# First layers of a mixture of experts that end at 8-token steps inside unchanged tiles

## The chip, the core and the metric

The kernel is one program on one core of a Trainium2 chip. The metric is the device time of a launch in microseconds, the median of several runs. On a core, TensorE (PE in the profile, its weight loads PEld) multiplies matrices, VectorE (DVE), ScalarE (ACT) and GpSimd (POOL) do the rest, SyncE (SP) issues most transfers. Each engine works through its own queue in order.

## The reference

Attention over a window of 128 tokens and 4 sink tokens (4 batches, 8 heads, 768 tokens, head size 64) gives 3072 token rows of 512 numbers. Each row then goes to one of 16 experts, picked in two steps (a group of 4, then one of 4 in it), and comes out scaled by the product of two softmax weights:

```python
g_idx = np.argmax(x @ w_group, axis=1)
e_idx = np.argmax(xg @ w_expert[g], axis=1)
h = np.maximum(xg[mask_e] @ w1[g, e], 0.0)      # 512 -> 1024
ye = h @ w2[g, e]                                # 1024 -> 512
out[tok_idx] = combined[:, None] * ye
```

All of it is float32. On the inputs drawn, the experts get 382, 244, 475, 275, 270, 204, 188, 163, 157, 156, 150, 134, 108, 92, 54 and 20 tokens in the order of ranks that the kernel uses: rank 0 and rank 1 are picked early, from a part of the tokens; the others follow by falling count.

## The kernel before, in words

**Two phases.** Up to some 185 us the kernel computes attention and routing, and it begins the first expert. From there on it works through the experts, one group of `GROUPS` (L52) after another. This text is on the second phase.

**Capacities.** Rank r has room for `CAPT[r]` tokens (L47), multiples of 32. Its tokens are gathered by index from a table in memory (unused places point at row 0), turned by TensorE and kept as columns of the tile `xx`, a rounded part and a residual, T columns each, one behind the other. Stores are scattered by index; unused places have an index out of bounds and are not written. If an expert has more tokens than `capt`, the flag `nov` sends the excess to `overflow` (L1493), a loop behind the main work that reads whole weights again for each tile of up to 128 tokens.

**First layer (`layer1_wide`, L974).** For each of 8 slices f of the hidden units and 4 slices c of the input, the weights (`hi`, a rounded part, and `lo`, the residual; `whi` and `wlo` in the profile) are the stationary operand of 128 columns, and the tokens are the moving operand. So the tokens are what is streamed: T columns. Every matmul brings its own weight load. With T of 240 or more there are three matmuls for each f and c: hi with the rounded tokens, hi with the residual tokens, lo with the rounded tokens, 96 in all. With T below 240 (`comb`, L976) the first two are one matmul over 2T columns, for the two token parts lie side by side: 32 pairs of one matmul of 2T columns with `hi` and one of T with `lo`. ScalarE and VectorE then add the halves (`hc`), and split the result after the ReLU into two parts again (`split_h`, L955).

**Second layer (`layer2`, L1106).** Here the hidden values are the stationary operand (w columns, at most 128) and the weights are what is streamed: 512 columns, whatever w is. In the ranks of `FEW` (3, 4, 8, 9, 10, 11) the last 32 tokens go another way: `few_tokens` (L1089) multiplies them unsplit (`hq`), four stationary tiles of 32 columns side by side.

**What sets the order.** A planner that runs while the program is built (`spend`, `wjob`, `routing`) keeps a model clock and puts the conversions of weights (ScalarE makes `whi`, VectorE makes `wlo`, for each chunk of 512 KB) between the other work. `split_h` tells it how long VectorE takes, by the number of columns (`dve(0.1 + T / 960)`). The order is then fixed. Weights are fetched by SP into nine buffers, and SP waits for each to come free.

**Stages.** The first layers lie in the trace of before as follows, from the span's start in us: rank 1 at 193.06, rank 8 at 218.40, rank 2 in two parts (256 columns at 235.23, 224 at 258.53), rank 9 at 280.18, rank 3 at 297.26, rank 10 at 332.42, rank 4 at 350.15, rank 5 at 381.75, rank 11 at 404.31, rank 6 at 421.98, rank 7 at 454.29.

Of the kernel before, what the change touches and what calls it, by code (L numbers as in the profile page):

```python
# [9 lines left out]
F32 = mybir.dt.float32  # L10
# [4 lines left out]
AF = mybir.ActivationFunctionType  # L15
ALU = mybir.AluOpType
# [5 lines left out]
P = 128  # L22
# [4 lines left out]
DM = H * D  # L27
# [4 lines left out]
NFC = F // P  # L32
# [30 lines left out]
HC = 3  # L63
# [16 lines left out]
for _g in PARTS:  # L80
    _o = 0
    for _q in _g:
        _rem = _q["T"] % P
        _m = _q["T"] - _rem if _q["r"] in FEW else _q["T"]
        _q.update(o=_o, nt=(_q["T"] + P - 1) // P, s=_rem if _rem <= 64 and _m == _q["T"] else 0, plain=_q["T"] <= 64, m=_m)
# [59 lines left out]
def moe_attention(tc, kqT, vN, vS, nsw, wgx, w1, w2, out):  # L145
    nc = Pinned(tc)
    v = nc.vector
    with ExitStack() as top, ExitStack() as att:
# [167 lines left out]
        def late_consts():  # L316
            for t in sacc:
                nc.gpsimd.memset(t[:, :, :, 1], 1e-9)
            nc.gpsimd.memset(rdt, 1e-9)
            other_masks()  # L320
            nc.sync.dma_start(wsb, wgx.rearrange("(c p) n -> p c n", p=P))
            for j in range(2):
                nc.sync.dma_start(wsd[j * D:(j + 1) * D, :, j],
                                  wgx.rearrange("(c j p) n -> j p c n", j=2, p=D)[j])
            for r in range(NE):
                nc.gpsimd.memset(capt[:, r:r + 1], float(CAPT[r]))
                nc.gpsimd.memset(caps[:, r:r + 1], float(CAPT[r] // P))

        def tables():
            v.tensor_scalar(colm, col, -float(P), None, ALU.add)  # L330
# [622 lines left out]
                v.tensor_copy(gate[0:w], src[p:p + w, DM:DM + 1])  # L953

        def split_h(q, fs, src):  # L955
            T, o, s, m = q["T"], q["o"], q["s"], q["m"]
            hi = hx[:, fs, o:o + m]
            nc.scalar.activation(hi, src[..., 0:m], AF.Relu)
            dve(0.1 + T / 960)
            yield  # L960
            if m < T:
                v.tensor_scalar(q["hq"][:, fs], src[..., m:T], 0.0, None, ALU.max)
            for a, z, d in ((0, m - s, m + s), (m - s, m, s)):
# [8 lines left out]
            return wt[k]  # L972

        def layer1_wide(q):  # L974
            T, o, r = q["T"], q["o"], q["r"]
            comb = T < 240  # L976
            lag = []
            if q["m"] < T:
                q["hq"] = yp.tile([P, NFC, 32], F32, name="hq", bufs=2)
            for f in range(NFC):  # L980
                ph = ps_h.tile([P, 512], F32, name="ph")
                fs = slice(f * P, (f + 1) * P)
                for c in range(NDC):
                    hi, lo = weights(1, r, c)
                    st, sp = c == 0, c == NDC - 1
                    if comb:
                        if sp:
                            nc.tensor.matmul(ph[:, 0:T], lo[:, fs], xx[:, c, o:o + T], start=False, stop=False)
                        nc.tensor.matmul(ph[:, 0:2 * T], hi[:, fs], xx[:, c, o:o + 2 * T], start=st, stop=sp)
                        if not sp:  # L990
                            nc.tensor.matmul(ph[:, 0:T], lo[:, fs], xx[:, c, o:o + T], start=False, stop=False)
                    else:
                        nc.tensor.matmul(ph[:, 0:T], hi[:, fs], xx[:, c, o:o + T], start=st, stop=False)
                        nc.tensor.matmul(ph[:, 0:T], hi[:, fs], xx[:, c, o + T:o + 2 * T], start=False, stop=False)
                        nc.tensor.matmul(ph[:, 0:T], lo[:, fs], xx[:, c, o:o + T], start=False, stop=sp)
                src = ph[:, 0:T]
                if comb:
                    src = yp.tile([P, 224], F32, name="hc", bufs=HC)[:, 0:T]
                    nc.scalar.copy(src, ph[:, T:2 * T])
                    v.tensor_tensor(src, ph[:, 0:T], src, ALU.add)  # L1000
                lag.append(split_h(q, f, src))
                if len(lag) > 1:
                    drain(lag[0])
                    lag.pop(0)
                next(lag[-1]) if not comb else None
                us = T / 200 + (0.24 if comb else 0.18)
                pop_todo()
                state["freed"] += 4 if q["last"] and f == NFC - 1 else 0
                yield us
            drain(lag[0])  # L1010
# [5 lines left out]
                    raise RuntimeError("weights out of order")  # L1016
            return held[k][0]

        def side_by_side(outs, w, n, xs, ws, chunk):
            m = P // w  # L1020
            for k in range(0, n, m):
                kk = range(k, min(n, k + m))
                for u, out in enumerate(outs):
                    for j, c in enumerate(kk):
                        nc.tensor.matmul(out[j * w:(j + 1) * w], xs(c), ws(c, u), start=k == 0, stop=k + m >= n)
# [80 lines left out]
        def layer2(q, j):  # L1106
            T, o, s, r, m = q["T"], q["o"], q["s"], q["r"], q["m"]
            w = min(P, T - j * P)
            st = w if j * P + w > T - s else 0
            po = ps_o.tile([P, DM], F32, name="po")  # L1110
            lastj = (j + 1) * P >= m
            end = q is PARTS[-1][-1] and j == 0
# [12 lines left out]
                    yield from rest  # L1125
            for f in range(0 if end else NFC):
                whi, wlo = (t[:, (f % 2) * DM:(f % 2 + 1) * DM] for t in weights(2, r, f // 2))
                hh = hx[:, f, o + j * P:o + j * P + w]
                a, z = f == 0, f == NFC - 1
                if st:  # L1130
                    hb = hx[:, f, o + j * P:o + j * P + 2 * w]
                    if z:
                        nc.tensor.matmul(po[0:w], hh, wlo, start=False, stop=False)
                    nc.tensor.matmul(po[0:2 * w], hb, whi, start=a, stop=z)
                    if not z:
                        nc.tensor.matmul(po[0:w], hh, wlo, start=False, stop=False)
                else:
                    hl = hx[:, f, o + m + s + j * P:o + m + s + j * P + w]
                    nc.tensor.matmul(po[0:w], hh, whi, start=a, stop=False)
                    nc.tensor.matmul(po[0:w], hh, wlo, start=False, stop=False)  # L1140
                    nc.tensor.matmul(po[0:w], hl, whi, start=False, stop=z)
                state["freed"] += 1 if q["last"] and lastj and f % 2 else 0
                if rest is None or f > RUN:
                    pop_todo()
                yield 0.467 if st else 0.7
                if rest and f == RUN:
                    pop_front()
                    yield from rest
            jj = q["j0"] + j
            ot = yp.tile([P, DM], F32, name="ot", bufs=3)  # L1150
            c = cg[r, jj]
            if end:
                for u in range(2):
                    nc.scalar.activation(ot[:, u * DM // 2:(u + 1) * DM // 2], pb[u][:, 0:DM // 2], AF.Copy, scale=c)
            else:
                nc.scalar.activation(ot[0:w], po[st:st + w], AF.Copy, scale=c[0:w])
            if st:
                v.scalar_tensor_tensor(ot[0:w], po[0:w], c[0:w], ot[0:w], ALU.mult, ALU.add)
            scatter(r, jj, w, ot)

        def rest_of(q):
            po = spare()
            yield from few_tokens(q, po, q["hq"], 32, q["j0"] + q["nt"] - 1)

        def fetch(nxt):
            for q in nxt:
# [458 lines left out]
```

## Time and profile before

| | us |
|---|---|
| time before, median of 3 runs | 490.12 (489.51 to 490.43) |
| the profiled execution, its own time | 492.94 |
| its span, first to last instruction | 491.2 |
| busy TensorE matmul / weight load | 472.3 / 395.9 |
| busy VectorE / ScalarE / GpSimd | 375.9 / 330.7 / 167.0 |

The granted TensorE clock is 0.997 of its full level. Busy time counts a matmul up to its modelled end, and matmuls overlap: the time that one takes in a stream is read from the start of the stage to the start of the next, divided by the count. Where a wait is put down to an engine, that engine was the last to release it.

### The profile page before, as it was taken

The page shows a single profiled execution, that of the slowest core. Times are in us where ns is not written, and L with a number is a line of the kernel's source. Part 1 is how long each engine was busy: PE and PEld are TensorE (multiplying, and loading weights), DVE is VectorE, ACT ScalarE, POOL GpSimd, SP SyncE. Part 2 cuts the span into 40 slices and gives each one's busy share as a digit, 9 for nine tenths or more (in the row PEclk, how much of TensorE's full clock was granted, in tenths as well). Part 3 has the DMA queues.
Part 4 walks back from the last instruction along what each step waited for, and adds up shares of the span by engine and source line. Part 5 has one row for each costly group of instructions (what it writes and reads, how often), then busy time and mean ns, then how long its engine had stood idle before and what let it go on. Part 6 is the DMA issues. An engine that isn't in the chain of part 4 may idle for free. (4 is left out here: it accounts for less than half of the span.)

```text
span 491.2 us, 14716 instructions
## 1 busy us (share of the span) xinstructions
PE 472.3 (96%) x5437; PEld 395.9 (81%) x5437; DVE 375.9 (77%) x1178; ACT 330.7 (67%) x858; POOL 167.0 (34%) x266
## 2 busy tenths in 40 slices
PE   8999999989989999999999999999999999999994
PEld 7788888877778888888989789668876978887974
DVE  6576888889898989887824876487587997999750
ACT  4999999878894535676615765367455787687751
POOL 3674665754663122312313123122131173103201
PEclk9999999999999999999999999999999999999998
DMA  8688889879968837753962347696949982999301
GB/s 241 183 279 274 264 244 266 262 243 324 297 190 282 315 105 253 266 175 115 381 239 83 107 172 246 217 326 248 329 164 380 403 312 76 366 387 355 116 9 43
DMA packets 59874, 117.09 MB, mean 238 GB/s; under 512 B 9758, under 2 KB 22046, under 8 KB 59792
## 3 DMA queue, kind: packets, MB, share of 16 engines
q1 hardware_dynamic: 54960, 102.50, 61.3%
q0 software_dynamic: 4304, 13.26, 8.1%
q8 instruction: 45, 0.74, 0.6%
q10 hardware_dynamic: 528, 0.29, 0.3%
q14 instruction: 37, 0.30, 0.2%
HBM read 103.25 MB, written 13.24 MB: 237 GB/s over the span
## 5 line engine op out<-in xcount | busy, mean ns | idle before, releaser
L115 DVE TENSOR_TENSOR wlo<-rw,whi 128x1024 fp32r<-128x1024 f32 x112 | 134.6, 1221 | 25.8 <-ACT whi L115 24.2
L115 PE MATMUL ph<-un,whi 128*128 128x256 f32 (+4 forms) x576 | 131.5, 316 | 1.2 <-DVE un L115 1.1
L115 PE MATMUL po<-whi,un 128*128 128x512 f32 (+2 forms) x384 | 127.9, 396 | 0.0
L115 POOL DMA_INDIRECT out<-ot,sidx x33 | 43.3, 1313 | 237.0 <-ACT ot L115 97.2
L115 ACT CAST whi<-rw 128x1024 fp32r<-128x1024 f32 (+1 forms) x115 | 115.4, 1025 | 10.7 <-PE po L115 6.9
L115 PE MATMUL ph<-un,wlo 128*128 128x160 f32 (+4 forms) x416 | 100.6, 266 | 0.1
L115 PEld LDWEIGHTS ph<-un,whi 128*128 128x128 f32 x576 | 94.1, 189 | 3.7 <-DVE un L115 1.4
L115 PEld LDWEIGHTS po<-whi,un 128*128 128x128 f32 (+1 forms) x384 | 70.8, 186 | 24.8 <-issue 6.7
L115 ACT ACTIVATE pt<-sm,st 128x136 f32<-128x136 f32 x192 | 76.1, 402 | 7.1 <-DVE st L115 6.1
L115 PEld LDWEIGHTS ph<-un,wlo 128*128 128x128 f32 x416 | 77.1, 189 | 1.2 <-DVE wlo L115 0.4
L115 PE MATMUL po<-wlo,un 128*128 128x512 f32 (+3 forms) x200 | 77.6, 389 | 0.0
L115 DVE CUSTOM_DVE_ANT_0 sm<-ps,msk 128x136 f32<-128x136 f32 x192 | 45.8, 295 | 8.0 <-PE ps L115 1.7
L115 PE MATMUL ps<-kb,qb 64*64 64x208 f32 (+1 forms) x768 | 40.0, 336 | 4.2 <-issue 3.9
L115 PEld LDWEIGHTS po<-wlo,un 128*128 128x128 f32 (+2 forms) x200 | 36.4, 182 | 7.4
L115 POOL DMA_INDIRECT xg<-xd,gidx x30 | 33.4, 1113 | 24.3 <-DVE sidx L115 11.6
L115 DVE TENSOR_TENSOR hc<-ph,hc 128x160 f32<-128x160 f32 (+2 forms) x64 | 21.8, 345 | 22.4 <-ACT hc L115 19.6
L115 POOL COPY pu<-spT 32x512 f32<-32x512 f32 x46 | 28.8, 652 | 25.3 <-ACT spT L115 24.2
L115 ACT ACTIVATION_READ_ACCUMULATOR pt<-sm,st 128x1 f32 x192 | 36.9, 192 | 0.0
L115 PEld LDWEIGHTS ps<-kb,qb 64*64 64x64 f32 x768 | 27.1, 134 | 10.6 <-issue 5.6
L115 ACT ACTIVATE ot<-po,cg 128x512 f32<-128x512 f32 (+3 forms) x25 | 17.0, 679 | 27.4 <-PE po L115 24.8
L115 ACT ACTIVATE un<-ph 128x256 fp32r<-128x256 f32 x40 | 15.3, 385 | 27.0 <-PE ph L115 25.4
L115 POOL TENSOR_SCALAR_AFFINE_SELECT pu<-pa 64x512 f32<-64x512 f32 x40 | 26.1, 652 | 19.6 <-ACT pa L115 19.6
(199 smaller groups left out, 723.7 us busy)
## 6 DMA issues: line engine op xcount, KB each, us to landing
rw<-in_w SPq DMA_DIRECT2D x128, 512.0 KB
vv<-in_vN SPq DMA_DIRECT2D x24, 512.0 KB
kb<-in_kqT SPq DMA_DIRECT2D x23, 288.0 KB
qb<-in_kqT SPq DMA_DIRECT2D x24, 256.0 KB
xd<-xt SPq DMA_DIRECT2D x24, 256.0 KB
vv<-in_vS SPq DMA_DIRECT2D x24, 128.0 KB
out<-ot,sidx POOLq DMA_INDIRECT x33, 9.1
xg<-xd,gidx POOLq DMA_INDIRECT x30, 5.2
```

What stands on the lines that cost most here:

```text
L115: r = f(*a, **k)
```

## The change

A second table `COLS` says how many columns of a rank are computed; `CAPT` stays and still sets the tiles, their places, the gathers and the planner's rules. For seven ranks COLS is smaller, on a step of 8:

| rank | 1 | 3 | 4 | 5 | 7 | 10 | 11 |
|---|---|---|---|---|---|---|---|
| tile (CAPT) | 256 | 288 | 288 | 224 | 192 | 160 | 160 |
| columns (COLS) | 248 | 280 | 272 | 208 | 168 | 152 | 136 |
| tokens | 244 | 275 | 270 | 204 | 163 | 150 | 134 |

The first layer's matmuls, the operations on their results, the stationary tiles of the second layer, the scaled output and the scatter all end at COLS. The limits in `capt` and `caps` that decide on overflow follow. In the `comb` form the two token parts now have a gap between them (T stays, n is smaller), so the moving operand has two pieces.

```diff
+COLS = [384, 248, 480, 280, 272, 208, 192, 168, 160, 160, 152, 136, 128, 128, 64, 32]
...
-        _q.update(o=_o, nt=...)
+        _q.update(o=_o, n=_q["T"] - (CAPT[_q["r"]] - COLS[_q["r"]] if _q["last"] else 0), nt=...)
...
-                nc.gpsimd.memset(capt[:, r:r + 1], float(CAPT[r]))
-                nc.gpsimd.memset(caps[:, r:r + 1], float(CAPT[r] // P))
+                nc.gpsimd.memset(capt[:, r:r + 1], float(COLS[r]))
+                nc.gpsimd.memset(caps[:, r:r + 1], float(COLS[r] // P))
...
         def split_h(q, fs, src):
-            T, o, s, m = q["T"], q["o"], q["s"], q["m"]
-            hi = hx[:, fs, o:o + m]
-            nc.scalar.activation(hi, src[..., 0:m], AF.Relu)
+            T, o, s, m = q["n"], q["o"], q["s"], q["m"]
+            e = min(m, T)
+            hi = hx[:, fs, o:o + e]
+            nc.scalar.activation(hi, src[..., 0:e], AF.Relu)
             dve(0.1 + T / 960)
...
         def layer1_wide(q):
-            T, o, r = q["T"], q["o"], q["r"]
+            T, n, o, r = q["T"], q["n"], q["o"], q["r"]
             comb = T < 240
...
+                    xh, xl = xx[:, c, o:o + n], xx[:, c, o + T:o + T + n]
                     if comb:
+                        both = xx[:, c, o:o + 2 * T].rearrange("p (k t) -> p k t", k=2)[:, :, 0:n]
...
-                        nc.tensor.matmul(ph[:, 0:2 * T], hi[:, fs], xx[:, c, o:o + 2 * T], start=st, stop=sp)
+                        nc.tensor.matmul(ph[:, 0:2 * n].rearrange("p (k t) -> p k t", k=2), hi[:, fs], both, start=st, stop=sp)
...
-                        nc.tensor.matmul(ph[:, 0:T], hi[:, fs], xx[:, c, o:o + T], start=st, stop=False)
-                        nc.tensor.matmul(ph[:, 0:T], hi[:, fs], xx[:, c, o + T:o + 2 * T], start=False, stop=False)
-                        nc.tensor.matmul(ph[:, 0:T], lo[:, fs], xx[:, c, o:o + T], start=False, stop=sp)
+                        nc.tensor.matmul(ph[:, 0:n], hi[:, fs], xh, start=st, stop=False)
+                        nc.tensor.matmul(ph[:, 0:n], hi[:, fs], xl, start=False, stop=False)
+                        nc.tensor.matmul(ph[:, 0:n], lo[:, fs], xh, start=False, stop=sp)
...
         def layer2(q, j):
...
+            n = min(w, q["n"] - j * P)
...
-                    nc.tensor.matmul(po[0:2 * w], hb, whi, start=a, stop=z)
+                    nc.tensor.matmul(po[0:w + n], hb, whi, start=a, stop=z)
...
         def rest_of(q):
-            yield from few_tokens(q, po, q["hq"], 32, q["j0"] + q["nt"] - 1)
+            yield from few_tokens(q, po, q["hq"], 32, q["j0"] + q["nt"] - 1, q["n"] - q["m"])
```

On TensorE, where rank 5's second layer ends and rank 11's first begins (`un` holds `xx` and `hx`; the last two numbers are stationary or output partitions and moving columns), the program of before has

```order
L115 MATMUL po_6700<-wlo_6517,un_87 96x512
L115 MATMUL po_6700<-whi_6516,un_87 96x512
L115 MATMUL ph_6747<-un_87,whi_6546 128x320
L115 MATMUL ph_6747<-un_87,wlo_6547 128x160
L115 MATMUL ph_6747<-un_87,whi_6566 128x320
L115 MATMUL ph_6747<-un_87,wlo_6567 128x160
L115 MATMUL ph_6747<-un_87,whi_6614 128x320
L115 MATMUL ph_6747<-un_87,wlo_6615 128x160
```

and the changed one, at the same place of the queue,

```order
L116 MATMUL po_6700<-wlo_6517,un_87 80x512
L116 MATMUL po_6700<-whi_6516,un_87 80x512
L116 MATMUL ph_6747<-un_87,whi_6546 128x272
L116 MATMUL ph_6747<-un_87,wlo_6547 128x136
L116 MATMUL ph_6747<-un_87,whi_6566 128x272
L116 MATMUL ph_6747<-un_87,wlo_6567 128x136
L116 MATMUL ph_6747<-un_87,whi_6614 128x272
L116 MATMUL ph_6747<-un_87,wlo_6615 128x136
```

No matmul has moved: the streamed columns of the first layer are fewer, those of the second stay at 512, and only its stationary columns are fewer. The same holds on VectorE and ScalarE, where the operations keep their places and lose columns. Only SP's queue has a shift, while it fetches weights for the first experts (`eidi` are the experts' numbers that it reads into registers, `rw` the buffers for weights): before

```order
L693 TENSOR_LOAD eidi_208
L693 ISA x2
L693 TENSOR_LOAD eidi_208
L693 ISA x2
L115 ISA
L115 DMA rw_4275<-in_w2 128x2x512
L115 ISA
L115 DMA rw_4298<-in_w2 128x2x512
L693 TENSOR_LOAD eidi_208
L693 ISA x2
L115 ISA
L115 DMA rw_4349<-in_w1 128x1024
```

and now

```order
L694 TENSOR_LOAD eidi_208
L694 ISA x2
L694 TENSOR_LOAD eidi_208
L694 ISA x2
L694 TENSOR_LOAD eidi_208
L694 ISA x2
L116 ISA
L116 DMA rw_4275<-in_w2 128x2x512
L116 ISA
L116 DMA rw_4298<-in_w2 128x2x512
L116 ISA
L116 DMA rw_4349<-in_w1 128x1024
```

One read of a register has moved ahead of two weight transfers.

## Rows read from the trace of the kernel before

**Rows 1.** The page: busy us, share of the span, instructions of each engine.

```profile
PE 472.3 (96%) x5437; PEld 395.9 (81%) x5437; DVE 375.9 (77%) x1178; ACT 330.7 (67%) x858; POOL 167.0 (34%) x266
```

**Rows 2.** Busy time by stretches: stretch, its us, engines (instructions), PE clock, DMA share, GB/s.

```profile
193.06:206.22 13.16, 12.17 (x98) 11.47 (x96) 11.55 (x41) 7.75 (x13) 5.69 (x5) 1.00 0.78 271
235.23:246.54 11.31, 11.31 (x97) 11.30 (x96) 8.75 (x13) 7.13 (x12) 4.61 (x3) 1.00 1.03 397
252.75:258.29 5.54, 5.54 (x25) 4.50 (x24) 0.00 (x0) 0.69 (x1) 1.01 (x1) 1.00 0.14 53
258.53:268.61 10.08, 10.08 (x66) 9.59 (x65) 4.53 (x13) 4.84 (x14) 3.87 (x4) 1.00 0.35 101
280.18:288.44 8.26, 8.26 (x65) 8.26 (x64) 6.20 (x21) 4.92 (x15) 3.09 (x3) 1.00 0.53 190
297.26:310.15 12.89, 12.89 (x97) 12.72 (x96) 8.03 (x18) 7.13 (x12) 5.14 (x5) 1.00 0.69 236
332.42:341.04 8.62, 8.52 (x66) 8.29 (x64) 6.38 (x19) 6.43 (x17) 0.94 (x1) 1.00 0.72 283
350.15:362.94 12.79, 12.79 (x98) 12.62 (x96) 7.92 (x18) 7.21 (x12) 3.76 (x3) 1.00 0.77 286
381.75:392.19 10.44, 10.32 (x65) 9.58 (x64) 9.70 (x16) 7.65 (x17) 1.09 (x1) 1.00 1.03 409
404.31:412.58 8.27, 8.27 (x66) 8.27 (x64) 5.69 (x18) 4.69 (x15) 4.09 (x4) 1.00 0.36 104
454.29:463.41 9.12, 9.12 (x65) 9.12 (x64) 7.26 (x22) 6.39 (x16) 2.64 (x2) 1.00 0.44 156
463.41:484.90 21.49, 21.49 (x121) 18.08 (x120) 10.12 (x16) 10.30 (x16) 1.91 (x2) 1.00 0.06 18
```

**Rows 3.** Waits of the weight loads from 192 to 492: us, times, longest.

```profile
PEld ph L115 <- DVE un L115: 1.1, 1, 1.1
PEld ph L115 <- DVE hc L115: 0.7, 2, 0.4
PEld ph L115 <- DVE wlo L115: 0.4, 1, 0.4
```

**Rows 4.** Timeline of weight loads in rank 9's first layer: start us, us, what.

```profile
283.43 0.19 PEld L115 LDWEIGHTS ph<-un,whi 128*128 128x128 f32 x1
283.54 0.19 PEld L115 LDWEIGHTS ph<-un,wlo 128*128 128x128 f32 x1
283.69 0.19 PEld L115 LDWEIGHTS ph<-un,whi 128*128 128x128 f32 x1
283.79 0.19 PEld L115 LDWEIGHTS ph<-un,wlo 128*128 128x128 f32 x1
```

**Rows 5.** Groups by form, whole span: rows*columns held, partitions x moving columns, count, us, mean ns.

```profile
L115 PE MATMUL po<-whi,un 128*128 128x512 f32 x336 | 114.9, 402 | 0.0
L115 PE MATMUL po<-whi,un 128*96 128x512 f32 x32 | 10.3, 393 | 0.0
L115 PE MATMUL ph<-rw,hq 128*32 128x512 f32 x96 | 11.5, 598 | 0.0
L115 PE MATMUL lg<-oh,trib 128*128 128x96 bf16 x3 | 0.7, 217 | 0.0
L115 PE MATMUL lg<-runb,onesb 128*128 128x96 bf16 x3 | 0.6, 202 | 0.0
```

**Rows 6.** VectorE's groups by form, 190 to 492: count, us, mean ns, idle before.

```profile
L115 DVE TENSOR_TENSOR hc<-ph,hc 128x160 f32<-128x160 f32 x32 | 10.0, 321 | 7.1 <-ACT hc L115 5.5 <-issue 1.6
L115 DVE TENSOR_TENSOR hc<-ph,hc 128x224 f32<-128x224 f32 x16 | 6.1, 388 | 13.5 <-ACT hc L115 12.3 <-issue 1.1
```

**Rows 7.** SP's reads of registers at line 693: ns min/median/max, first and last us.

```profile
L693 SPq TENSOR_LOAD <-eidi x14: 15/270/281, 181.8 to 200.8; - x14
```

**Rows 8.** Timeline of VectorE and ScalarE ahead of rank 5's first layer: start us, us, what.

```profile
374.47 1.05 ACT L115 CAST whi<-rw 128x1024 fp32r<-128x1024 f32 x1 [1.48 <-DMA rw<-in_w]
380.57 4.61 DVE L115 TENSOR_TENSOR wlo<-rw,whi 128x1024 fp32r<-128x1024 f32 x4
```

More of the change, by code (lines that the diff above doesn't have):

```diff
@@ L84 @@
         _m = _q["T"] - _rem if _q["r"] in FEW else _q["T"]
-        _q.update(o=_o, nt=(_q["T"] + P - 1) // P, s=_rem if _rem <= 64 and _m == _q["T"] else 0, plain=_q["T"] <= 64, m=_m)
+        _q.update(o=_o, n=_q["T"] - (CAPT[_q["r"]] - COLS[_q["r"]] if _q["last"] else 0), nt=(_q["T"] + P - 1) // P, s=_rem if _rem <= 64 and _m == _q["T"] else 0, plain=_q["T"] <= 64, m=_m)
         _o += 0 if _q["plain"] else 2 * _q["T"]
@@ L961, in split_h @@
             if m < T:
-                v.tensor_scalar(q["hq"][:, fs], src[..., m:T], 0.0, None, ALU.max)
-            for a, z, d in ((0, m - s, m + s), (m - s, m, s)):
+                v.tensor_scalar(q["hq"][:, fs, 0:T - m], src[..., m:T], 0.0, None, ALU.max)
+            for a, z, d in ((0, min(m - s, e), m + s), (m - s, e, s)):
                 if z > a:
@@ L974, in layer1_wide @@
         def layer1_wide(q):
-            T, o, r = q["T"], q["o"], q["r"]
+            T, n, o, r = q["T"], q["n"], q["o"], q["r"]
             comb = T < 240
             lag = []
-            if q["m"] < T:
+            if q["m"] < n:
                 q["hq"] = yp.tile([P, NFC, 32], F32, name="hq", bufs=2)
@@ L985, in layer1_wide @@
                     st, sp = c == 0, c == NDC - 1
+                    xh, xl = xx[:, c, o:o + n], xx[:, c, o + T:o + T + n]
                     if comb:
+                        both = xx[:, c, o:o + 2 * T].rearrange("p (k t) -> p k t", k=2)[:, :, 0:n]
                         if sp:
-                            nc.tensor.matmul(ph[:, 0:T], lo[:, fs], xx[:, c, o:o + T], start=False, stop=False)
-                        nc.tensor.matmul(ph[:, 0:2 * T], hi[:, fs], xx[:, c, o:o + 2 * T], start=st, stop=sp)
+                            nc.tensor.matmul(ph[:, 0:n], lo[:, fs], xh, start=False, stop=False)
+                        nc.tensor.matmul(ph[:, 0:2 * n].rearrange("p (k t) -> p k t", k=2), hi[:, fs], both, start=st, stop=sp)
                         if not sp:
-                            nc.tensor.matmul(ph[:, 0:T], lo[:, fs], xx[:, c, o:o + T], start=False, stop=False)
+                            nc.tensor.matmul(ph[:, 0:n], lo[:, fs], xh, start=False, stop=False)
                     else:
-                        nc.tensor.matmul(ph[:, 0:T], hi[:, fs], xx[:, c, o:o + T], start=st, stop=False)
-                        nc.tensor.matmul(ph[:, 0:T], hi[:, fs], xx[:, c, o + T:o + 2 * T], start=False, stop=False)
-                        nc.tensor.matmul(ph[:, 0:T], lo[:, fs], xx[:, c, o:o + T], start=False, stop=sp)
-                src = ph[:, 0:T]
+                        nc.tensor.matmul(ph[:, 0:n], hi[:, fs], xh, start=st, stop=False)
+                        nc.tensor.matmul(ph[:, 0:n], hi[:, fs], xl, start=False, stop=False)
+                        nc.tensor.matmul(ph[:, 0:n], lo[:, fs], xh, start=False, stop=sp)
+                src = ph[:, 0:n]
                 if comb:
-                    src = yp.tile([P, 224], F32, name="hc", bufs=HC)[:, 0:T]
-                    nc.scalar.copy(src, ph[:, T:2 * T])
-                    v.tensor_tensor(src, ph[:, 0:T], src, ALU.add)
+                    src = yp.tile([P, 224], F32, name="hc", bufs=HC)[:, 0:n]
+                    nc.scalar.copy(src, ph[:, n:2 * n])
+                    v.tensor_tensor(src, ph[:, 0:n], src, ALU.add)
                 lag.append(split_h(q, f, src))
@@ L1017, in whole, with side_by_side @@
             return held[k][0]
-        def side_by_side(outs, w, n, xs, ws, chunk):
+        def side_by_side(outs, w, n, xs, ws, chunk, u=None):
             m = P // w
+            wx = u or w
             for k in range(0, n, m):
@@ L1024, in side_by_side @@
                     for j, c in enumerate(kk):
-                        nc.tensor.matmul(out[j * w:(j + 1) * w], xs(c), ws(c, u), start=k == 0, stop=k + m >= n)
+                        nc.tensor.matmul(out[j * w:j * w + wx], xs(c), ws(c, u), start=k == 0, stop=k + m >= n)
                 for c in kk:
@@ L1087, in layer2_plain, with few_tokens @@
             yield from few_tokens(q, spare(), q["h"], q["T"], 0)
-        def few_tokens(q, po, h, T, jj):
+        def few_tokens(q, po, h, T, jj, n=None):
             r = q["r"]
-            yield from side_by_side([po], T, NFC, lambda f: h[:, f],
-                                    lambda f, u: whole(2, r, f // 2)[:, (f % 2) * DM:(f % 2 + 1) * DM], lambda f: (2, r, f // 2))
+            n = n or T
+            yield from side_by_side([po], T, NFC, lambda f: h[:, f, 0:n],
+                                    lambda f, u: whole(2, r, f // 2)[:, (f % 2) * DM:(f % 2 + 1) * DM], lambda f: (2, r, f // 2), n)
             c = cg[r, jj]
             ot = yp.tile([P, DM], F32, name="ot", bufs=3)
-            nc.scalar.activation(ot[0:T], po[T:2 * T], AF.Copy, scale=c[0:T])
+            nc.scalar.activation(ot[0:n], po[T:T + n], AF.Copy, scale=c[0:n])
             for a in [a for a in range(0, P, T) if a != T]:
-                v.scalar_tensor_tensor(ot[0:T], po[a:a + T], c[0:T], ot[0:T], ALU.mult, ALU.add)
-            scatter(r, jj, T, ot)
+                v.scalar_tensor_tensor(ot[0:n], po[a:a + n], c[0:n], ot[0:n], ALU.mult, ALU.add)
+            scatter(r, jj, n, ot)
         def scatter(r, jj, w, ot):
@@ L1127, in layer2 @@
                 whi, wlo = (t[:, (f % 2) * DM:(f % 2 + 1) * DM] for t in weights(2, r, f // 2))
-                hh = hx[:, f, o + j * P:o + j * P + w]
+                hh = hx[:, f, o + j * P:o + j * P + n]
                 a, z = f == 0, f == NFC - 1
                 if st:
-                    hb = hx[:, f, o + j * P:o + j * P + 2 * w]
+                    hb = hx[:, f, o + j * P:o + j * P + w + n]
                     if z:
-                        nc.tensor.matmul(po[0:w], hh, wlo, start=False, stop=False)
-                    nc.tensor.matmul(po[0:2 * w], hb, whi, start=a, stop=z)
+                        nc.tensor.matmul(po[0:n], hh, wlo, start=False, stop=False)
+                    nc.tensor.matmul(po[0:w + n], hb, whi, start=a, stop=z)
                     if not z:
-                        nc.tensor.matmul(po[0:w], hh, wlo, start=False, stop=False)
+                        nc.tensor.matmul(po[0:n], hh, wlo, start=False, stop=False)
                 else:
[L1138 to L1141, printed above, removed]
+                    hl = hx[:, f, o + m + s + j * P:o + m + s + j * P + n]
+                    nc.tensor.matmul(po[0:n], hh, whi, start=a, stop=False)
+                    nc.tensor.matmul(po[0:n], hh, wlo, start=False, stop=False)
+                    nc.tensor.matmul(po[0:n], hl, whi, start=False, stop=z)
                 state["freed"] += 1 if q["last"] and lastj and f % 2 else 0
@@ L1155, in layer2 @@
             else:
-                nc.scalar.activation(ot[0:w], po[st:st + w], AF.Copy, scale=c[0:w])
+                nc.scalar.activation(ot[0:n], po[st:st + n], AF.Copy, scale=c[0:n])
             if st:
-                v.scalar_tensor_tensor(ot[0:w], po[0:w], c[0:w], ot[0:w], ALU.mult, ALU.add)
-            scatter(r, jj, w, ot)
+                v.scalar_tensor_tensor(ot[0:n], po[0:n], c[0:n], ot[0:n], ALU.mult, ALU.add)
+            scatter(r, jj, n, ot)
         def rest_of(q):
             po = spare()
-            yield from few_tokens(q, po, q["hq"], 32, q["j0"] + q["nt"] - 1)
+            yield from few_tokens(q, po, q["hq"], 32, q["j0"] + q["nt"] - 1, q["n"] - q["m"])
         def fetch(nxt):
```

## The prediction

> **What bounds the kernel now.** I read the page's busy times first, then the stages of the second phase one by one, then the waits, and the weight loads at single steps. The page gives TensorE 472.3 us of matmul in a span of 491.2, VectorE 375.9, ScalarE 330.7 [rows 1]: the end hangs on TensorE, as long as the others keep it fed. The stages show how far that holds. In the first layers of ranks 9, 3, 4, 11 and 7 and in both parts of rank 2, TensorE is busy for the whole stretch (8.26 of 8.26, 12.89 of 12.89, and so on), at a granted clock of 1.00, which is its level of 2.4 GHz [rows 2]. Three stages have holes: rank 1 (12.17 of 13.16), rank 10 (8.52 of 8.62) and rank 5 (10.32 of 10.44); their loads wait for a PSUM tile that VectorE frees (`un`, 1.1 us), for `hc` and for `wlo` (0.4 us) [rows 3]. From 463.41, where the last changed stage ends, to 484.90 there is none (21.49 of 21.49) [rows 2]. So a column that is not streamed shortens the kernel if it was on TensorE's path inside its stage.
>
> **What a column costs.** Whether it was on that path is the question of this case, for a stage needs two things of TensorE: streaming the tokens, and loading 128 columns of weights for every matmul. Take the `comb` stages, 32 pairs each [rows 2]: 320+160 columns take 8.26 and 8.27 us (258.3 ns a pair), 384+192 take 9.12 (285.0), 448+224 take 10.08 (315.0). From the first to the last, 128 columns with `whi` and 64 with `wlo` come on top, and 56.7 ns. That is 0.443 ns for each `whi` column and nothing for those with `wlo`; if all 192 counted, a column would cost 0.295 ns. Which reading holds is told by the larger matmuls. With three equal matmuls in 96, 288 columns take 12.89 and 12.79 us (133.7 ns each), 256 take 11.31 (117.8), and 512, in the second layer, 5.54 us for 24 (230.8) [rows 2]: 0.497 ns a column between 256 and 288, 0.434 from 288 to 512. So a streamed column costs 0.43 to 0.50 ns, and the `wlo` columns of the pairs cost none: they lie beside something else. That is the weight load: inside a pair, the load of `wlo` starts 0.11 us after that of `whi` (283.43 to 283.54), the next `whi` 0.15 us later, 0.10 us before the `wlo` behind it [rows 4]. Two loads never start closer than that, and 160 columns at 0.44 ns are 71 ns. A pair is then one load (some 113 ns with what comes around it: 258.3 less 320 by 0.443 is 117, 315.0 less 448 by 0.443 is 117) and the streaming of `whi`.
>
> The Trainium skill says the same of the load, in "TensorE: Matmul & The Clock Gate", section "LDWEIGHTS (loading the stationary operand)": it takes the number of columns divided by 1.2, in ns, so 106.7 ns for 128 columns, whatever the rows. By that rule a matmul with fewer than 256 streamed columns is set by its load, and rank 1, from 256 to 248, would win nothing; the trace's 0.10 to 0.11 us between loads agree [rows 4], and with rank 1 at zero the sum below would be 3.0 us in place of 3.1.
>
> **The change, part by part.**
>
> *First layers in pairs.* `whi` loses 32 columns in rank 5 (448 to 416), 48 in rank 7 (384 to 336), 16 in rank 10 (320 to 304), 48 in rank 11 (320 to 272). By 32 matmuls and 0.443 ns: 0.45, 0.68, 0.23 and 0.68 us, together 2.04. The 24 to 8 columns that `wlo` loses in each I cost at nothing, for the load covers them; were that cover not there, they would give 72 by 32 by 0.443, 1.02 us more. Rank 11 at 272 and 136 lies below the shortest row (320); 272 columns at 0.443 are 120 ns, still more than a load, so the line holds.
>
> *First layers in threes.* Rank 3 loses 8 columns in 96 matmuls, rank 4 loses 16. By 0.434 to 0.497 ns that is 0.33 to 0.38 and 0.67 to 0.76 us; I take 0.47 ns: 0.36 and 0.72. Rank 1 loses 8 in 96: at most 0.38 us. Its nearest row is the stage at 256 columns, where the loader is busy 11.30 of 11.31 us [rows 2], so that little can come of streaming less, and its own stage waits 1.1 us for VectorE anyway [rows 3]. I take 0.1 and keep 0 and 0.38.
>
> *Two pieces.* 128 matmuls (four ranks, 32 each) now read their columns in two pieces with a gap. The trace has no such matmul in the second phase. The nearest rows are in the routing: six pieces of 16 columns (`runb`, broadcast) take 202 ns, 96 columns in one piece 217 [rows 5]. So I cost the pieces at nothing; the other end is a rival below.
>
> *Second layers.* They stream 512 columns as before. 96 stationary columns take 393 ns, 128 take 402 [rows 5]; 120, 80, 104 and 40 in their place change no streaming, and a shorter load lies under it (4.50 us of loads in 5.54) [rows 2]. `few_tokens` keeps four tiles of 512 streamed columns (598 ns each at 32 columns [rows 5]); 24, 16 and 8 columns hold fewer outputs and stream the same. Zero for both; a part of the 9 ns between the two rows of the second layer is the most that either could give or take.
>
> *VectorE and ScalarE.* `hc` takes 321 ns at 160 columns and 388 at 224 [rows 6], 1.05 ns a column: with 8 to 24 columns less in 32 such operations some 0.6 us fewer over four ranks, on an engine that is not the bound. I count nothing for it; it is cover for the waits. Stores of 8 to 24 rows fewer leave out rows that were not written before.
>
> *SP.* One register read (270 ns [rows 7]) now stands ahead of two weight transfers of 512 KB, near 200 us, and delays them by about that. At the 397 GB/s of a busy stretch [rows 2] such a transfer alone takes 1.3 us, and it is fetched ahead of its use. Zero.
>
> *Waits.* TensorE reaches the next weights earlier. Where they are late already, the gain is given back, unless the chain that makes them starts from TensorE too. At rank 5 (382.9) it does: the casts behind it begin with a transfer that landed at 374.47, after a wait, and VectorE's four `wlo` run from 380.57 [rows 8]; these transfers are issued when TensorE has freed buffers, behind rank 4's first layer, and so they move ahead with it. At rank 1 and 10 the wait is for VectorE's work on the same stage. I keep 0.1 us as lost.
>
> The sum is 2.04 + 0.36 + 0.72 + 0.1 - 0.1 = 3.1 us. Of the profiled execution (492.94 us, span 491.2) that leaves 489.8 and a span of 488.1; it is 0.63%, and from the median of the runs, 490.12, it leaves 487.0 us. Its own range, with 0.43 or 0.50 ns a column and rank 1 at either end, is 2.8 to 3.8 us, so 486.3 to 487.3, and with the spread of the runs before (0.5 either way) 485.8 to 487.8.
>
> **Rivals.**
>
> *Every column counts.* 9,984 columns are left out in all. At 0.45 ns, between the prices above, that is 4.5 us: 485.6. For it: from 384+192 to 448+224 a pair grows by 30.0 ns, a little more than 64 `whi` columns give (28.4). Against it: over the whole way from 320+160 the `wlo` columns add nothing [rows 2]. The skill's isolated rule on the same page, "Back-to-back issue gap" (columns by 2.4 plus 2.5 ns), would give 4.2 us, 486.0, but it states itself that it counts too little where columns are few.
>
> *The waits take it.* If weights or PSUM tiles arrive by VectorE's and ScalarE's own pace, what is won up to rank 5's wait (0.1 + 0.36 + 0.23 + 0.72 = 1.4) is waited off there, and only ranks 5, 11 and 7 keep theirs: 1.8 us, 488.3. For it: VectorE is busy 9.70 of 10.44 us in rank 5 and 11.55 of 13.16 in rank 1 [rows 2]. Against it: these waits are short, and the chain starts from TensorE.
>
> *The second piece costs.* If the matmul over two pieces runs as two, each held to the time of a load, a triple takes 339 ns (three times 113) where I expect 237, 251, 264 and 301 ns in ranks 11, 10, 7 and 5: 102 + 88 + 75 + 38, by 32, are 9.7 us more and, less 3.1, 6.6 us slower: 496.7. It decides from 24 ns for a second piece on (3.1 us by 128). Against it: the rows of the broadcast operand.
>
> *A rank overflows.* The new limits leave 2 to 5 free places. One token more than a limit would start the overflow loop; its weights alone, 4 MB, at the 397 GB/s of the busiest stretch [rows 2] are over 10 us: 497 or more. The counts in the reference's own arithmetic all fit.
>
> **Chances and range.** My forecast 0.70; every column 0.08; the waits 0.15; the second piece 0.05; overflow 0.02. A measurement of this kernel can tell 0.2%, about 1 us, from no change. The forecast, every column and three fifths of the case with waits (0.09) lie beyond it: faster 0.87; the rest of the waits, 0.06, within; slower 0.07. The range reaches from every column (485.6) to the waits (488.3) with the runs' spread: 485.4 to 488.8.
>
> **What would show it.** In the profile after: rank 11's first layer at 7.5 to 7.6 us, rank 7's at 8.4, rank 4's at 12.1, rank 5's near 10.0; 32 pairs of 272+136 at 237 ns; rank 1's at 12.8 to 13.2; loads again 0.10 to 0.11 us apart at the closest; the stretch behind the last first layer unchanged at 21.5 us. Were rank 11's stage near 7.2 us, every column counted; if TensorE's holes in ranks 1, 10 and 5 grow by over 1 us together, the waits took it; if a pair of 272+136 takes 258 ns or more, the pieces cost. A branch into the overflow loop, or a first layer that is longer than before, would make the prediction wrong.

## The result, and the profile after

The changed kernel took 485.56 us (median of 6 runs, 484.62 to 487.44) beside 490.27 us of the kernel before on the same chip: a ratio of 0.9904 [0.9875, 0.9933], 4.7 us less. Two later comparisons gave 0.9921 [0.9882, 0.9960] and 0.9920 [0.9889, 0.9951], 3.9 us less each. The prediction was 487.0 us, 3.1 us less than the 490.12 us it started from, in a range of 485.4 to 488.8.

The page's busy times of the kernel after answer to [rows 1]: TensorE has 3.8 us less matmul, VectorE 2.2 less, and the span is 485.3 in place of 491.2.

```profile
PE 468.5 (97%) x5437; PEld 391.9 (81%) x5437; DVE 373.7 (77%) x1178; ACT 330.2 (68%) x858; POOL 166.8 (34%) x266
```

The stages, kernel after, busy time by stretches (columns as in [rows 2]); from the top the first layers of ranks 1, 3, 10, 4, 5, 11 and 7, then all behind the last of them:

```profile
190.50:202.36 11.86, 11.74 (x97) 11.10 (x96) 11.55 (x41) 7.83 (x13) 5.69 (x5) 1.00 0.85 290
293.22:305.59 12.37, 12.37 (x98) 12.21 (x96) 7.85 (x18) 7.14 (x12) 4.78 (x5) 1.00 0.68 236
327.85:336.93 9.08, 8.58 (x66) 8.14 (x64) 6.30 (x19) 5.98 (x17) 2.30 (x2) 1.00 0.66 258
346.02:358.06 12.04, 12.04 (x97) 11.89 (x95) 7.60 (x18) 7.11 (x12) 3.65 (x4) 1.00 0.82 303
376.88:386.91 10.03, 9.86 (x65) 9.56 (x64) 9.27 (x15) 7.46 (x16) 0.88 (x1) 1.00 1.03 409
399.01:406.64 7.63, 7.63 (x66) 7.62 (x64) 5.91 (x21) 4.78 (x15) 4.07 (x4) 1.00 0.37 110
448.30:456.82 8.52, 8.52 (x66) 8.52 (x65) 6.67 (x21) 6.03 (x16) 3.14 (x2) 1.00 0.46 160
456.82:478.30 21.48, 21.48 (x121) 17.78 (x120) 10.17 (x16) 10.25 (x16) 1.94 (x2) 1.00 0.06 20
```

Set beside [rows 2], ranks 3, 4, 5, 11 and 7 give 0.52, 0.75, 0.41, 0.64 and 0.60 us; a pair of 272+136 takes 238 ns (7.63 us by 32), where 237 was forecast; the last stretch is the same. Two rows don't fit: rank 1 gave 1.30 us for 8 columns, and rank 10 became 0.46 longer though it streams less. The waits of the weight loads for VectorE, 186 to 490 us, answer to [rows 3]: the wait for `hc` has grown, the one for `un` shrunk.

```profile
PEld ph L116 <- DVE hc L116: 1.3, 3, 0.7
PEld ph L116 <- DVE un L116: 0.5, 2, 0.3
PEld ph L116 <- DVE wlo L116: 0.4, 1, 0.4
```

And a third: rank 1's first layer starts at 190.50 in place of 193.06, though all ahead of it is the same work. Three things were thus to be settled: what of rank 1 and rank 10 belongs to the columns, whether the load really covers `wlo`, and where the rest of the 4.7 us came from.

### The profile page after: what moved, and what is told of

Its sections match the earlier page's. It is cut to its first block, busy times and chain, and to the rows that moved or that the text cites. A ratio compares the mean times of both kernels' runs of the same rounds, so it can differ in the third digit from the quotient of the medians.

```text
span 485.3 us, 14716 instructions
## 1 busy us (share of the span) xinstructions
PE 468.5 (97%) x5437; PEld 391.9 (81%) x5437; DVE 373.7 (77%) x1178; ACT 330.2 (68%) x858; POOL 166.8 (34%) x266
## 5 line engine op out<-in xcount | busy, mean ns | idle before, releaser
L116 PE MATMUL ph<-un,whi 128*128 128x256 f32 (+9 forms) x576 | 128.5, 312 | 1.3 <-DVE un L116 0.6
L116 PE MATMUL po<-whi,un 128*128 128x512 f32 (+5 forms) x384 | 127.8, 396 | 0.0
L116 PE MATMUL ph<-un,wlo 128*128 128x256 f32 (+10 forms) x416 | 99.3, 263 | 0.2 <-DVE wlo L116 0.2
L116 PEld LDWEIGHTS po<-whi,un 128*128 128x128 f32 (+4 forms) x384 | 70.3, 184 | 25.2 <-issue 6.7
L116 PE MATMUL po<-wlo,un 128*128 128x512 f32 (+6 forms) x200 | 77.5, 389 | 0.0
L116 PEld LDWEIGHTS po<-wlo,un 128*128 128x128 f32 (+5 forms) x200 | 36.0, 180 | 7.6
L116 DVE TENSOR_TENSOR hc<-ph,hc 128x160 f32<-128x160 f32 (+6 forms) x64 | 21.1, 335 | 21.5 <-ACT hc L116 21.5
L116 ACT ACTIVATE ot<-po,cg 128x512 f32<-128x512 f32 (+6 forms) x25 | 17.0, 680 | 27.4 <-PE po L116 27.3
L116 ACT ACTIVATE un<-ph 128x256 fp32r<-128x256 f32 (+1 forms) x40 | 15.3, 384 | 24.6 <-PE ph L116 23.8
```

The lines of the kernel that those rows point to most:

```text
L116: r = f(*a, **k)
```

## The experiments

### Both kernels again, rank 1 alone, and all but rank 1

No edit in two of them; in the other two only the table of columns, set against the kernel after:

```diff
-COLS = [384, 248, 480, 280, 272, 208, 192, 168, 160, 160, 152, 136, 128, 128, 64, 32]
+COLS = [384, 248, 480, 288, 288, 224, 192, 192, 160, 160, 160, 160, 128, 128, 64, 32]   # rank 1 alone
+COLS = [384, 256, 480, 280, 272, 208, 192, 168, 160, 160, 152, 136, 128, 128, 64, 32]   # all but rank 1
```

The kernel before again: 

> The kernel before, profiled once more. Theory A (chance): the 1.1 us hole of rank 1's first layer is of that one execution, in which ScalarE learned of a finished tile 3.4 us late; now the stage takes 11.6 to 12.3 us in place of 13.15. Theory B (the columns): the hole belongs to the 256 columns; 13.0 to 13.3 again. Both: 490.1 us, within 0.1% of the kernel before. Rank 10's first layer 8.6 us again if its wait is fixed by the order of the work.

Rank 1 alone: 

> Only rank 1 at 248 columns, all other ranks as before. Theory A: only the streaming is won; undisturbed matmuls fall from 117.8 to 114.3 ns, by 96 that is 0.34 us, ratio 0.9993. Theory B: the hole closes with it, 1.3 us, ratio 0.9974. The forecast on record (the load covers the stream there) had 0.1 us, ratio 0.9998.

All but rank 1: 

> All ranks at their new columns but rank 1, which stays at 256. Theory A: 0.3 us less is won than by the whole change: ratio 0.991. Theory B: 1.3 us less is won: ratio 0.993. Rank 1's first layer: A 11.5 to 12.3 us, B 13.0 to 13.3. Ranks 4, 11, 7, 5 as in the changed kernel: 12.04, 7.63, 8.52, 10.03.

The kernel after again: 

> The changed kernel, profiled once more. Ratio 0.990 to 0.993. Rank 10's first layer: 8.3 to 8.5 us if its grown hole (0.9 us) came of a transfer that was late in one execution, 9.0 to 9.2 again if the order of the work brings it. Rank 1's start within 1 us of 190.5 if the first 190 us differ by chance only.

Times: 0.9995 [0.9957, 1.0033], 0.9998 [0.9959, 1.0037], 0.9889 [0.9827, 0.9951] and 0.9921 [0.9882, 0.9960]. Rank 1 alone can't be told from no change, and all but rank 1 can't be told from the whole change; both intervals hold what either theory named, so the times don't decide. The stages do. Rank 1's first layer in the kernel before, again (the first row; the second is its rank 10):

```profile
191.69:203.99 12.30, 12.19 (x97) 11.48 (x96) 11.48 (x41) 7.97 (x13) 5.71 (x5) 1.00 0.84 285
330.20:338.45 8.25, 8.25 (x66) 8.25 (x64) 6.73 (x21) 6.13 (x17) 1.01 (x2) 1.00 0.70 273
```

the same in the kernel with rank 1 alone at 248 columns (again rank 1, then rank 10):

```profile
193.11:206.18 13.07, 12.00 (x97) 11.18 (x96) 11.41 (x41) 7.71 (x13) 5.67 (x5) 1.00 0.83 271
332.24:341.50 9.26, 8.78 (x65) 8.33 (x64) 6.37 (x19) 6.37 (x17) 1.75 (x2) 1.00 0.71 280
```

in the kernel after, again:

```profile
190.32:203.36 13.04, 12.02 (x97) 11.18 (x96) 11.40 (x41) 7.70 (x13) 5.69 (x5) 1.00 0.81 266
328.85:337.66 8.81, 8.32 (x65) 8.09 (x64) 6.30 (x19) 6.00 (x17) 1.72 (x2) 1.00 0.69 270
```

and rank 1 with all but rank 1 cut:

```profile
189.96:202.27 12.31, 12.18 (x98) 11.50 (x97) 11.47 (x41) 7.96 (x13) 5.68 (x5) 1.00 0.84 284
```

The reader is to look at the first number of each row: 256 columns took 13.15, 12.30 and (all but rank 1) 12.31 us, 248 took 11.86, 13.07 and 13.04. A wait of about 1.1 us for VectorE's `un` is there or not, whatever the columns, in the same kernel too. Theory B falls: rank 1's 1.30 us are 0.33 us of streaming (undisturbed matmuls fall from 117.8 to 114.4 ns, 96 of them) and chance. Rank 10 is the same: 8.62 and 8.25 in the kernel before, 9.08 and 8.81 in the one after, and 9.26 with its old 160 columns; the 8.81 lie between the two cases that had been named (8.3 to 8.5, 9.0 to 9.2). Ranks 3, 11 and 7 repeat to 0.01 us at the same columns in these six traces; rank 4 does but for one trace (12.77 in place of 12.04, with all but rank 1), in which TensorE waits 0.5 us in one place.

### Only the wlo columns cut

Against the kernel before; the second edit stands twice in the kernel and is shown once:

```diff
+            L = 32 if r in (5, 7, 10, 11) else T
-    nc.tensor.matmul(ph[:, 0:T], lo[:, fs], xx[:, c, o:o + T], start=False, stop=False)
+    nc.tensor.matmul(ph[:, 0:L], lo[:, fs], xx[:, c, o:o + L], start=False, stop=False)
```

> The kernel before, with all wlo matmuls of the first layers of ranks 5, 7, 10 and 11 over 32 columns in place of 224, 192, 160 and 160 (the rest of that product is left out). Theory A (the load covers the wlo columns): the four stages stay at 10.2 to 10.4, 9.1, 8.2 to 9.3 and 8.3 us. Theory B (all streamed columns count alike; the pairs, always two to one, fit 0.295 ns for each of them as well): shorter by 192, 160, 128 and 128 columns in 32 matmuls, 1.8, 1.5, 1.2 and 1.2 us: 8.5, 7.6, 7.1 and 7.1 us.

This kernel, the next one and the one after that were timed once each, so only their stages are read.

Its first layers of ranks 10, 5, 11 and 7 (in the last, one matmul of a second layer, 0.23 us, has slipped in between):

```profile
333.00:341.45 8.45, 8.45 (x65) 8.25 (x64) 6.46 (x19) 5.79 (x17) 1.07 (x2) 1.00 0.70 272
382.37:392.47 10.10, 10.10 (x66) 9.58 (x64) 9.37 (x15) 7.61 (x16) 1.00 (x1) 1.00 1.03 410
404.58:412.84 8.26, 8.26 (x65) 8.26 (x64) 6.20 (x21) 4.92 (x15) 4.09 (x4) 1.00 0.37 104
454.52:463.89 9.37, 9.37 (x66) 9.32 (x65) 7.37 (x22) 6.39 (x16) 3.25 (x2) 1.00 0.43 150
```

Rank 11 loses 128 of 160 columns in 32 matmuls and takes 8.26 us where [rows 2] have 8.27. Theory B wanted 7.1. Rank 5 is 0.1 to 0.3 us shorter than in the three traces with the same columns (10.44, 10.32 and 10.21 us), whose waits for `wlo` of 0.2 to 0.4 us it doesn't have; no stage gives more. So the `wlo` columns cost nothing: what a pair takes beside `whi`'s stream is a floor. That the floor is the load's is seen in the loads themselves, kernel with short `wlo`, rank 11 (start us, us, what; loads first):

```profile
404.73 0.19 PEld L115 LDWEIGHTS ph<-un,whi 128*128 128x128 f32 x1
404.84 0.19 PEld L115 LDWEIGHTS ph<-un,wlo 128*128 128x128 f32 x1
404.99 0.19 PEld L115 LDWEIGHTS ph<-un,whi 128*128 128x128 f32 x1
```

```profile
404.73 0.18 PE L115 MATMUL ph<-un,wlo 128*128 128x32 f32 x1
404.76 0.39 PE L115 MATMUL ph<-un,whi 128*128 128x320 f32 x1
404.99 0.18 PE L115 MATMUL ph<-un,wlo 128*128 128x32 f32 x1
```

Two matmuls are recorded 0.03 us apart here, while no two loads of this stage start closer than 0.108 us. Nor is the floor a price of every matmul: in the attention phase of the kernel before, 250 matmuls and 254 loads, most of them of 64 columns and some side by side, pass in 9.00 us:

```profile
95.00:104.00 9.00, 9.00 (x250) 8.10 (x254) 8.09 (x47) 8.43 (x34) 6.33 (x11) 1.00 0.86 275
```

No run changed how many columns are held, so that the floor goes with the 128 of them is not shown.

### The equal matmuls below 256 columns

Against the kernel before, cut to what matters:

```diff
+SHORT = {1: 160, 3: 240, 4: 208}
+    k = SHORT.get(r, T)     # columns of all but the first of 12 matmuls
```

> The kernel before, with 11 of 12 matmuls of the equal kind cut: rank 3 from 288 to 240 columns, rank 4 from 288 to 208, rank 1 from 256 to 160 (the rest of the product is left out). Theory A (a matmul takes its load or its stream, the longer): a floor of 107 to 113 ns, so rank 4 at 10.5 to 11.0 us and rank 1 at 10.4 to 10.9 and its waits; rank 3 at 10.8 to 11.0. Theory B (streaming alone, 0.45 ns a column): rank 3 at 10.8, rank 4 at 9.5, rank 1 at 7.5 and its waits.

Its first layers of ranks 1, 3 and 4:

```profile
191.92:203.67 11.75, 11.46 (x98) 10.87 (x96) 11.44 (x41) 7.81 (x13) 5.69 (x5) 1.00 0.86 297
294.76:305.84 11.08, 11.08 (x99) 10.96 (x97) 7.40 (x17) 7.13 (x12) 4.67 (x4) 1.00 0.64 226
345.47:357.11 11.64, 11.60 (x97) 11.09 (x96) 7.07 (x16) 6.86 (x12) 4.06 (x3) 1.00 0.83 307
```

Rank 4 at 208 columns takes longer than rank 3 at 240, and more than theory A's 10.5 to 11.0: three of its last tiles start late, which costs some 0.7 us in all; without that it would be near 11.0. Rank 3 is 0.08 above what both theories named. The widths are told apart better between such waits. One matmul takes, start to start (the mean of the third to the eleventh of each twelve; the second, behind the longer first, is left out, for it takes as little as 75 ns at 160 columns):

| columns | 288 | 272 | 256 | 248 | 244 | 240 | 208 | 160 |
|---|---|---|---|---|---|---|---|---|
| ns | 133 | 124.4 | 117.8 | 114.4 | 113.1 | 112.9 | 111.5 | 111.6 |

From 288 to 244 a column is worth 0.45 ns, from 240 to 160 next to nothing (1.3 ns in 80 columns). Theory A holds, with the bend near 244: rank 1 at 248 still stands on the steep side.

### One piece in place of two

The edit in words, against the kernel after:

```diff
-    whi's columns: xx[o:o+n] and xx[o+T:o+T+n]
+    whi's columns: xx[o:o+2*n], the residuals written at o+n   # ranks 5, 7, 10, 11
```

> The changed kernel, with the residual columns of ranks 5, 7, 10 and 11 packed right behind the others, so that whi reads one piece. Theory A (the second piece costs nothing): rank 11 at 7.63, rank 7 at 8.52 us as in the changed kernel, within 0.05. Rival (a piece costs): shorter, by 0.03 us for every ns of a second piece.

Ranks 11 and 7, first layers:

```profile
397.30:404.89 7.59, 7.59 (x65) 7.58 (x64) 5.94 (x21) 4.78 (x15) 4.06 (x4) 1.00 0.35 110
446.56:455.09 8.53, 8.53 (x65) 8.52 (x64) 6.59 (x21) 6.01 (x16) 3.13 (x2) 1.00 0.43 156
```

0.04 us less and 0.01 more: a second piece costs between -0.3 and 1.3 ns. Nothing, as forecast.

### Columns down to the tokens, and the kernel after a third time

The counts of tokens, rounded up to even numbers:

```diff
-COLS = [384, 248, 480, 280, 272, 208, 192, 168, 160, 160, 152, 136, 128, 128, 64, 32]
+COLS = [382, 244, 476, 276, 270, 204, 188, 164, 158, 156, 150, 134, 128, 128, 64, 32]
```

> The changed kernel with its columns cut on to the tokens there are (even numbers): 382, 244, 476, 276, 270, 204, 188, 164, 158, 156, 150, 134. Theory A: 56 whi columns in 32 matmuls at 0.443 and 10 columns in 96 at 0.45 ns, 0.8 + 0.4 = 1.2 us less than the changed kernel, 4.4 to 5.0 us less than the kernel before: ratio 0.990 to 0.991 where the changed kernel has 0.992 to 0.993. Theory B (rank 1 is at its load already): 1.0 us. Rank 11 at 7.57, rank 7 at 8.40, rank 4 at 11.95, rank 6 at 9.35 us.

The kernel after: 

> The changed kernel on the same chip, to set the one before it against. Ratio 0.990 to 0.994; rank 3 at 12.37, rank 4 at 12.04, rank 11 at 7.63, rank 7 at 8.52 us; rank 1 between 11.6 and 13.1 and rank 10 between 8.0 and 9.2, by chance.

Times: 0.9932 [0.9902, 0.9961] and 0.9920 [0.9889, 0.9951]: no gain that can be measured, where 1.0 to 1.2 us had been expected. The stages without waits did shorten, in part by less than expected: rank 7 8.38 (0.13 less), ranks 2b and 9 0.10 each, rank 3 0.08, ranks 8, 6 and 11 0.07 to 0.04, rank 4 nothing. Rank 10, at 150 columns, took 9.57 us, 0.9 more than in the kernel after beside it; this time the wait took it.

### What rank 10 waits for, and casts that stand later

Ten of the traces so far show what the wait hangs on. In this stage ScalarE's queue holds `hc` of tile 1, a cast (`whi`), `hc` of tile 2; VectorE's `wlo` of that cast stands ahead of its own `hc`, which frees a PSUM tile. Set the cast's start, counted from the stage's start, beside TensorE's wait for `hc`:

| columns of rank 10 | 160 | 152 | 160 | 152 | 160 | 152 | 152 | 152 | 160 | 150 |
|---|---|---|---|---|---|---|---|---|---|---|
| cast starts at, us | 1.41 | 1.75 | 1.95 | 1.99 | 2.10 | 2.20 | 2.34 | 2.61 | 2.76 | 3.10 |
| wait for `hc`, us | 0 | 0.1 | 0.2 | 0.4 | 0.3 | 0.6 | 0.7 | 0.9 | 0.9 | 1.4 |

The wait follows the cast and not the columns, and from 1.95 us on the cast nearly always stands behind a transfer, as in the kernel after (timeline of ScalarE, then of VectorE: start us, us, what, and the idle time before it with what ended it):

```profile
329.05 0.29 ACT L116 COPY hc<-ph 128x152 f32<-128x152 f32 x1
330.46 1.05 ACT L116 CAST whi<-rw 128x1024 fp32r<-128x1024 f32 x1 [1.13 <-DMA rw<-in_w]
331.42 0.28 ACT L116 COPY hc<-ph 128x152 f32<-128x152 f32 x1
```

```profile
331.55 1.23 DVE L116 TENSOR_TENSOR wlo<-rw,whi 128x1024 fp32r<-128x1024 f32 x1 [1.75 <-ACT whi L116]
332.69 0.31 DVE L116 TENSOR_TENSOR hc<-ph,hc 128x152 f32<-128x152 f32 x1
```

A transfer reports its landing in sixteen parts. In this trace fifteen of this transfer's were there 0.93 us into the stage and the last at 2.54; in ten of all thirteen traces the last came 0.8 to 2.2 us behind the one before it, in the other three at most 0.34. Why one part is late was not settled.

The test leaves the columns alone and has the planner expect each transfer 0.5 us later, which puts this cast behind the second `hc` (and moves others):

```diff
-DMASLACK = 1.0
+DMASLACK = 1.5
```

> The changed kernel, its planner expecting each weight transfer 0.5 us later, so that in rank 10's first layer ScalarE's second cast (whi) stands behind the second hc and not ahead of it. Theory A (the hole is the second hc waiting behind a cast that waits for its transfer: in ten traces it is the cast's start, from the start of the stage, less 1.7 us): the hole of 0 to 0.9 us shrinks to at most 0.3, rank 10 at 8.0 to 8.4 us. Theory B (VectorE's wlo itself delays hc, wherever it stands): the hole only moves one tile on, rank 10 at 8.2 to 9.1 as before. Time: from 0.5 us less than the changed kernel to no difference, ratio 0.991 to 0.993.

With the columns of the tokens as well: 

> The columns cut to the tokens (0.5 to 1.2 us less streaming than the changed kernel) together with the casts 0.5 us later. Theory A: rank 10 at 7.9 to 8.4 us in place of 9.57, and 1 to 2 us less than the changed kernel: ratio 0.988 to 0.990. Theory B (the wait takes what streaming gives): rank 10 above 9 us, ratio 0.991 to 0.993.

ScalarE in the same place, kernel with later casts, and its rank 10:

```profile
327.34 0.28 ACT L116 COPY hc<-ph 128x152 f32<-128x152 f32 x1
328.34 0.29 ACT L116 COPY hc<-ph 128x152 f32<-128x152 f32 x1 [0.72 <-PE ph L116]
328.52 0.31 ACT L116 ACTIVATE un<-hc 128x128 fp32r<-128x128 f32 x1
328.73 1.04 ACT L116 CAST whi<-rw 128x1024 fp32r<-128x1024 f32 x1
```

```profile
326.13:334.17 8.04, 8.04 (x65) 8.03 (x64) 6.62 (x21) 6.22 (x17) 1.41 (x1) 1.00 0.75 294
```

The cast starts 2.60 us into the stage, as late as in the kernel after (2.61), and TensorE waits for nothing: 8.04 us in place of 9.08. But here it is its place that makes it late and not the transfer, which had landed at 2.01; by the table the old place would have cost 0.3 to 0.6 us with such a transfer. The sharper test is the kernel with the tokens' columns too, its cast and its rank 10:

```profile
330.92 1.05 ACT L116 CAST whi<-rw 128x1024 fp32r<-128x1024 f32 x1 [0.24 <-DMA rw<-in_w]
```

```profile
327.97:336.26 8.29, 8.29 (x66) 8.10 (x64) 6.51 (x20) 6.27 (x17) 0.93 (x1) 1.00 0.72 287
```

Its transfer is later than in nine of the ten traces: the cast waits for it and starts 2.95 us into the stage, where the table has waits of 0.9 (at 2.76) and 1.4 (at 3.10). TensorE waits 0.2 us, and the stage takes 8.29 in place of 9.57. It was the place in the queue that made a late transfer a wait. From rank 1's first matmul to the last of all, the traces take 291.9 and 290.9 us in the kernel before, 287.9, 289.5 and 287.3 in the one after, 286.5 with later casts and 286.1 with both. In time: 0.9928 [0.9900, 0.9956] and 0.9909 [0.9874, 0.9945], both faster than the kernel before, neither to be told from the kernel after; the 1 to 2 us that the second was expected to gain on it are not seen.

## Why the prediction was right, and what it mis-sized

*Pairs (2.04 us).* Right, a little high: ranks 11 and 7 gave 0.64 and 0.60 where 0.68 each was forecast. Ranks 5 and 10, whose stages hold waits, gave 0.47 and 0.21 without them: rank 5 by its undisturbed pairs (314.6 to 300.0 ns, by 32), rank 10 by the stages that waited for nothing (8.25 in the kernel before, again, and 8.04 with later casts); forecast were 0.45 and 0.23. In all 1.92. That `wlo` costs nothing was the argument's hinge; the run with `wlo` alone cut shows it.

*Threes (1.18 us).* Mis-sized. Rank 4 gave 0.75 (0.72 forecast), rank 3 0.52 (0.36), rank 1 0.33 (0.1): 1.60. Rank 3's stage took 0.10 us more than rank 4's at the same 288 columns (12.89 and 12.79 [rows 2]), and that went with the cut; why is not known. For rank 1 I took the matmul at 256 columns to be on its load already, because the loader was busy 11.30 of 11.31 us [rows 2]. A busy loader did not prove that; the bend is near 244. The Trainium skill ("TensorE: Matmul & The Clock Gate", section "LDWEIGHTS (loading the stationary operand)") has the load at 106.7 ns, by which rank 1 would win nothing. The loads here start 108 ns apart at the closest, which agrees, but in a stream of 160 columns one matmul takes 111.6, 5 ns more; and the 3.4 ns a matmul won from 256 to 248 columns are not nothing, so that here the measurement decides.

*Two pieces, `few_tokens`, last stretch.* Nothing, as forecast. The second layer of rank 1, costed at nothing with 9 ns a matmul as the bound, has a little: from its first layer's end to rank 8's, 12.18 us became 12.03 to 12.06 in each trace with 248 columns.

*Waits (0.1 us lost).* Not borne out as a size: rank 10's hole ran from 0 to 0.9 us with 160 columns and from 0.1 to 0.9 with 152, on the mean 0.3 and 0.5 in five traces each, too few to tell these apart; rank 1's, ahead of its last tile, from 0 to 1.1 with either kernel's. I had read one execution's holes as the kernel's; that they are drawn anew each time was not in the prediction. Two of its signs failed for that reason: rank 1's first layer took 11.86 us where 12.8 to 13.2 was named, and rank 10's was longer than before (9.08 and 8.62), which was named as a sign of being wrong. The repeats put both to the execution.

*The sum.* 1.92 + 1.60 and 0.15 in rank 1's second layer are 3.7 us, which repeat; 3.1 were forecast, 0.4 of the difference in the threes. The 3.1 us lie just outside the first comparison's interval (3.3 to 6.1) and inside the other two. The 3.7 lie inside all three: 1.0 below the first's 4.7 us, 0.2 below the 3.9 of the others. Of the 5.9 us between the two spans first profiled, 2.56 had passed ahead of any changed stage, by a stall told of below.

*The rivals.* "Every column counts" named 485.6 us, which is the time first measured, and it is wrong: its mechanism would have put rank 11's stage near 7.2 us, and that is 7.63. Only the stage tells them apart; the time alone would have chosen the wrong one. "The waits take it" was right in kind for rank 10, whose waits can eat its gain in an execution, and not in amount: rank 5's wait for `wlo`, where all that was won ahead of it would have been lost, is 0.3 and 0.4 us in the kernel before and 0.2 and 0.4 in the first two traces of the one after. "The second piece costs" and an overflow did not happen.

## What to carry to other kernels

In a stream of matmuls that each bring a load, one took the longer of its load (108 to 113 ns here) and its stream (0.45 ns a column), so columns are worth cutting only above the bend (here near 244 at 128 rows and columns held); ask it of the matmul's own neighbours, with stages of other widths in the same trace. Read a hole of half a microsecond from two executions before it enters a sum, and take a term from stages without holes. Where a queue holds a cast that may wait for a transfer, what stands behind it waits too: an instruction that frees a PSUM tile belongs ahead of it.

## What had not been expected of the hardware

In three of thirteen traces TensorE stood still for 2.6 to 3.1 us in the attention phase, waiting for nothing that the profile shows, while instructions were fetched. In the kernel before (timeline, then the DMA queues of 104.6 to 107.2 us):

```profile
107.18 0.46 PE L115 MATMUL ps<-kb,qb 64*64 64x136 f32 x6 [2.29 <-issue]
```

```profile
q8 instruction: 1, 0.02, 2.6%
```

The fetch began at 104.79 and took 1.08 us, less than the 2.57 us from one matmul's start to the next. Each trace has 93 to 96 such fetches, nearly all without a stall, so that the fetch is the cause is not shown. The ten other traces have no gap of TensorE above 1.6 us between 25 and 190 us. All three were traces in which most ranks had their old columns (three of five), none was among eight with the new ones. The instructions up to that point are the same, and the kernel before has it in one trace and not in the other, so I take it for chance; the runs don't prove it. One thing speaks against it: rank 1's first layer starts at 191.7 to 194.8 us in all five traces with most of the old columns and at 188.8 to 190.9 in all eight with the new ones. Were this of the columns, the whole change would give more than the 3.7 us of its stages; the three times (4.7, 3.9, 3.9) leave that open. Why PSUM tiles of rank 1 come free 1.1 us late in some executions was not settled either.
